# A fused attention and mixture-of-experts kernel: the order of eight row gathers, three table scatters, one table read and one weight load

## The chip, the cores and the metric

The kernel runs on one core of a Trainium2 chip. The metric is device time in microseconds, as the median of three runs. Engines are named as in the profile: PE is TensorE, DVE is VectorE, ACT is ScalarE, POOL is GpSimd, SP is SyncE, which only issues DMAs.

## What is computed

The first part is a retention layer: blockwise attention with a decay, over 4 batches, 8 heads, 768 positions and 64 channels. Its output is turned into `x`, 3072 rows of 512. The second part is a mixture of 8 experts in which every row goes to the one expert with the largest logit:

```python
logits = x @ w_gate
e_idx = np.argmax(logits, axis=1)
...
gate_w = probs[np.arange(N), e_idx]
eom = 1.0 / (1.0 + np.exp(-(x @ w_output_gate)))
for e in range(E):
    mask = e_idx == e
    h = np.maximum(x[mask] @ w1[e], 0.0)
    ye = h @ w2[e]
    out[mask] = gate_w[mask, None] * eom[mask, e, None] * ye
```

Which rows an expert gets is known only while the kernel runs, so the kernel sorts rows by expert in a table in DRAM and gathers them.

## The kernel before

**Attention and routing.** `x` is made in 24 tiles of 128 rows, by a software pipeline over steps s = -2 to 21 with the stages `stage_a` to `stage_d2`, and the last two tiles behind the loop. `stage_d2` turns a tile for DRAM and `store_x` sends two tiles at a time to `x_d` on SP's queue. Four tiles (the last four in two pairs) are routed together: `logits`, `route_choose` (which expert), `route_place` (which place in the table). For every tile `place_scatter` then writes 128 records of 12 bytes into the table `tab_d` with an indirect DMA from POOL. Each indirect DMA is made by POOL's own instruction (lines 712 and 969). `pace(t)` is a copy of one element on POOL that makes it wait for `t`, and `idle_for(2)`, a rest pair, two such copies of nothing in particular.

**The first expert.** After 16 tiles (`RES = 16`), the expert that has most rows so far is chosen, and its rows are worked on first, as "expert 0". Its rows among the first 16 tiles, the early rows, stand in the first 256 places of its list: eight gathers of 32 places each, in blocks 0 to 7, read from `x_d` into the tiles `xg(0, 0)` and `xg(0, 1)`. `x_turn(0, 0)` and `x_turn(0, 1)` transpose these on DVE, line 986, and PE's first expert products need them (`units`, issued by `fill`, line 1021: 16 units with the first tile, 16 with the second, 16 with both and the second half of the weights, `load_piece(1)`; then 16 units of second products with pieces 2 and 3, lines 84 to 86). Its places from 256 on, blocks 8 to 13, are shared between rows of the first 16 tiles, which come out of the table by `load_rows(0, 2)` (SP, line 869) and `row_index(0, 2)` (DVE, lines 897 and 902), and rows of the last 8 tiles, which PE finds by products with `marks` (`found`, lines 611 and 612; DVE, `row_turn` and `row_join`). The gathers 8 to 13 follow, and behind them those of expert 1, whose list is read by `load_rows(1)` and `row_index(1)` after all 24 scatters.

**What sets the order.** The block stands under `manual_schedule`: each engine, and each DMA queue, runs its instructions in the order of the program. The framework adds the waits from what is read and written. Accesses to `tab_d` are kept in program order among reads and scatters; scatters among themselves are declared free of order (`scatter`, line 722). On POOL, before the change: scatter of tile 12 (s = 17), gathers 0 and 1 (s = 18), 2 and 3 (s = 19), scatters of tiles 13 and 14 (s = 20), scatter of tile 15 and gather 4 (s = 21), gathers 5, 6 and 7 behind the loop, then the scatters of tiles 16 to 23 with a rest pair ahead of each, the gathers 8 to 13, and expert 1's. On SP: `load_piece(0)` (s = 19), stores, then at s = 21 `load_rows(0, 2)` and `load_piece(1)`, the last stores, `load_piece(2)` and `load_piece(3)`, `load_rows(1)`. On DVE, `row_index(0, 2)` stands ahead of the routing of the last two tiles and of `x_turn(0, 1)`; `row_index(1)` stands behind the split of the first quarter of piece 3 and ahead of its other three (lines 139 and 1470).

Of the kernel before, what the change touches and what calls it, by code (L numbers as in the profile page):

```python
# [25 lines left out]
def kernel(  # L26
# [17 lines left out]
    P = 128  # L44
# [31 lines left out]
    RES = 16  # L76
    def bank(name):
        return psum.tile([P, 512], F32, tag="bank", name=name)
# [627 lines left out]
    def place_scatter(count, rests=0):  # L706
        for _ in range(min(count, len(pending))):
            idx, rec = pending.pop(0)
            idle_for(rests)
            scatter(  # L710
                "table",
                nc.gpsimd.indirect_dma_start(  # L712
                    out=tab_d,
                    out_offset=bass.IndirectOffsetOnAxis(ap=idx, axis=0),
                    in_=rec,
                    in_offset=None,
                    bounds_check=P * E * EB - 1,
                    oob_is_err=False,
                ),
            )  # L720

    def scatter(group, ins):
        inst = getattr(ins, "ins", ins)
        tc.declare_no_dep(inst, group=group, reason="these scatters write different rows")
        tc.add_to_no_dep_group(group, inst)
# [137 lines left out]
    def load_rows(p, j0=0, j1=None, eng=nc.sync):  # L863
        if p >= E:
            return
        n = (KT[p] if j1 is None else j1) - j0
        t = const.tile([32, 4 * n, 3], I32, name=f"index_{p}_{j0}")
        src = tab_q[bass.ds(expert[p], 1)][:, :, 4 * j0 : 4 * (j0 + n), :]
        eng.dma_start(t, src.rearrange("e r j t -> (e r) j t"))
        idxs[(p, j0)] = (t, n)  # L870
# [17 lines left out]
    def idle_for(count):  # L888
        for _ in range(count):
            pace(warm[0:1])  # L890

    def row_index(p, j0=0):
        if p >= E:
            return
        t, n = idxs[(p, j0)]
        gf = const.tile([32, 4 * n], F32, name=f"rowf_{p}_{j0}")
        nc.vector.scalar_tensor_tensor(
            out=gf, in0=t[:, :, 2], scalar=float(4 * NT), in1=t[:, :, 2], op0=ALU.is_lt, op1=ALU.mult
        )
        gi = const.tile([P, 4 * n], I32 if p else F32, name=f"rows_{p}_{j0}")  # L900
        for qq in range(4):
            nc.vector.tensor_scalar(
                out=gi[32 * qq : 32 * qq + 32], in0=gf, scalar1=float(P * qq), scalar2=None, op0=ALU.add
            )
        if p == 0:
            part0[j0] = gi
            return
        for b in range(4 * n):
            gis[(p, 4 * j0 + b)] = gi[:, b : b + 1]
# [52 lines left out]
    def gather(p, b0=0, b1=None, rows=NT, rests=0):  # L962
        if p >= E:
            return
        for b in range(b0, NB[p] if b1 is None else min(b1, NB[p])):
            idle_for(rests)
            if (p, b // 4) not in xg:
                xg[(p, b // 4)] = slot(f"xg_{p}_{b // 4}")
            nc.gpsimd.indirect_dma_start(  # L969
                out=xg[(p, b // 4)][:, (b % 4) * P : (b % 4 + 1) * P],  # L970
                out_offset=None,
                in_=x_q[0 : 4 * rows],
                in_offset=bass.IndirectOffsetOnAxis(ap=gis[(p, b)], axis=0),
                bounds_check=4 * rows - 1,
                oob_is_err=False,
            )
# [301 lines left out]
    with tc.manual_schedule():  # L1278
# [13 lines left out]
        for s in range(-2, NTILE - 2):  # L1292
            if s >= 0:
                load_up_to(s + AHEAD - (s >= B), 2 if s < RES + 3 else 1)
            if s == -2:
                decay_table()
            if s == 0:
                stage_b(1)
                stage_b2(1)
            if s == RES + 1:  # L1300
                load_every()
            rest = stage_a(s + 2)
            if late:
                late.pop(0)()
            if s >= 1 and s % B == 0:
                logits(s - B, B)
            for f in rest:
                f()
            if s >= 0:
                stage_c1(s)  # L1310
            stage_a2(s + 2)
            if s + 1 >= 0 and s != 0:
                stage_b(s + 1)
            if s == RES + 2:
                pfound = bank("pfound")
                for b in range(B):
                    found(pfound, RES - B + b, 0, 2 * P, b == 0, b == B - 1)
                row_turn(0, pfound, 2 * P)
            n = s - 1
            if s >= 1 and s % B == 0:  # L1320
                logit_rows(s - B)
            if s + 1 >= 0 and s != 0:
                stage_b2(s + 1)
            if n >= 0 and n % B == B - 1:
                at_once(route_choose(n + 1 - B, n + 1))
                if n < RES:
                    pace(routed[n + 1 - B][0][0:1, 0, 0:1])
                else:
                    decay_queries(s + 2)
                ranking = route_place(n + 1 - B, n + 1)  # L1330
                per_turn[0] = 3 if n >= RES - 1 else 2
            if s == RES + 2:
                first_index()
                row_join(0, 2 * P)
            if s == RES + 5:
                decay_queries(s + 2)
            stage_k(s + 2)
            if s == RES + 1:
                weave(len(later))
                expert_regs(0, order_i, 1)  # L1340
            if s >= RES + 2:
                if s > RES + 2:
                    pace(live[s + 1]["at"][1][0:1, 0, 0:1])
                if s < RES + 4:
                    gather(0, 2 * (s - RES - 2), 2 * (s - RES - 2) + 1, RES * P)
                else:
                    place_scatter(1)
            if 0 <= n < LAST:
                stage_d2(n)
            if s in STORES:  # L1350
                store_x(STORES[s], 2)
            if s == 0:
                later.extend(inter_tables())
                routing_tables()
                order_tables()
            if s == 1:
                weave(len(later))
            if s == 2:
                nc.scalar.dma_start(wgs[:, :, 0:E], w_gate.rearrange("(c p) e -> p c e", p=P))
                nc.scalar.dma_start(wgs[:, :, E : 2 * E], w_output_gate.rearrange("(c p) e -> p c e", p=P))  # L1360
                blank_rows()
            if s == 5:
                number_tables()
            if s in EARLY_RECORDS:
                early_record(*EARLY_RECORDS[s])
            if s >= 0:
                stage_c(s)
            if s == RES + 3:
                decay_queries(s + 2)
            if ranking:  # L1370
                first_steps = pick_first() if s == RES else []
                late.append(lambda fs=first_steps[:1] + ranking[:1]: [f() for f in fs])
                place_scatter(len(pending) if s == RES else 0)
                later.extend(first_steps[1:] + ranking[1:-1])
                if s == RES:
                    later.extend(lambda b=b: mark(RES - B, b, 0, 2 * P) for b in range(B))
                later.extend(ranking[-1:])
                ranking = []
            if s == RES + 3:
                load_piece(0)  # L1380
            if s > RES:
                pace(xTs[s][0:1, 256:257])
                if s in (RES + 1, RES + 4):
                    place_scatter(1)
                elif s < RES + 4:
                    gather(0, 2 * (s - RES - 2) + 1, 2 * (s - RES - 2) + 2, RES * P, 2)
                else:
                    load_rows(0, 2)
                    load_piece(1)
                    gather(0, 4, 5, RES * P)  # L1390
            if s < RES:
                place_scatter(1 if s < RES - 2 else 2)

# [4 lines left out]
        weave(2)  # L1398
        stage_b2(n)
        pace(live[n]["at"][1][0:1, 0, 0:1])  # L1400
        gather(0, 5, 6, RES * P)
        stage_c(n - 1)
        pace(xTs[n - 1][0:1, 256:257])
        gather(0, 6, 7, RES * P)
        logits(LAST, 2)
        weave(len(later))
        for b in range(B):
            mark(RES, b, 1, late_width)
        gather(0, 7, 8, RES * P, 2)
        stage_c1(n)  # L1410
        logit_rows(LAST)
        stage_c(n)
# [11 lines left out]
            mark(LAST, b, 1, late_width)  # L1424
        stage_d2(n - 3, 2)
        fill(8)
        row_index(0, 2)
        logit_rows(LAST + 2)
        fill(8)
        at_once(route_choose(LAST + 2, NTILE))  # L1430
        x_turn(0, 1)
        stage_d2(n - 1, 2)
        load_piece(2)
        load_piece(3)
        last = route_place(LAST + 2, NTILE)
# [288 lines left out]
```

## Time and profile before

| | |
|---|---|
| median of 3 runs | 411.56 us (410.62 to 412.21) |
| the profiled execution's own time | 411.95 us |
| its span | 410.1 us |
| PE busy | 393.6 us, 96% |
| DVE, ACT, POOL busy | 289.0, 184.6, 245.7 us |
| chain that ended last | PE 77%, DMA 10%, SP's queue 6%, DVE 4% |

A row of the timeline gives the start, the length, the engine, the source line, the operation, what it writes and reads, the number of instructions merged into it and, in brackets, how long the engine sat idle just before and what ended that. A wait for several semaphores is put down to the one that came last by the profile; where the engine named had long been done, it was another, often a DMA. A granted clock of 1.00 is 2.4 GHz, 0.50 is 1.2 GHz.

### The profile page before, as it was taken

To read this page: it belongs to the slowest core of one execution; us is meant where nothing else is said; L and a number is where in the kernel's file an instruction comes from. 1 tells how busy PE (TensorE), PEld (TensorE's weight loads), DVE (VectorE), ACT (ScalarE), POOL (GpSimd) and SP (SyncE) were. 2 spreads that over 40 slices of the span, in tenths; PEclk is the share of its full clock that TensorE was granted. 3 is DMA by queue.
4 is the path that set the end of the run, shared out by engine and by line. 5 is a ranking of instruction groups with operands and counts; after the bars stand their busy time and mean duration, and the time that the engine had idled before them with its cause. 6 is when DMAs were issued, how large, how long until landed. Compare 5 with 4: busy or idle time off the path is not lost.

```text
span 410.1 us, 10897 instructions
## 1 busy us (share of the span) xinstructions
PE 393.6 (96%) x3847; PEld 368.6 (90%) x3847; DVE 289.0 (70%) x845; ACT 184.6 (45%) x450; POOL 245.7 (60%) x362
## 2 busy tenths in 40 slices
PE   7999999999959999999999999999999999999994
PEld 4888978888749899899999999999999999999984
DVE  3857686789964836875969858966976886875611
ACT  3767556687411504544435414704623642552500
POOL 2567886764876888686585656557466475403102
PEclk9999999999997999999999999999999999999999
DMA  9998999988867248754359646946965884783201
GB/s 183 226 208 209 246 252 241 258 223 207 270 185 245 58 164 258 229 197 144 129 167 307 225 141 197 307 144 180 320 214 151 270 301 135 229 318 111 71 26 49
DMA packets 106286, 81.99 MB, mean 200 GB/s; under 512 B 67028, under 2 KB 81386, under 8 KB 106210
## 3 DMA queue, kind: packets, MB, share of 16 engines
q1 hardware_dynamic: 97666, 67.52, 57.4%
q0 software_dynamic: 6288, 13.12, 10.0%
q8 instruction: 52, 0.85, 0.9%
q10 hardware_dynamic: 2256, 0.30, 0.5%
q14 instruction: 24, 0.20, 0.1%
HBM read 63.78 MB, written 17.55 MB: 198 GB/s over the span
## 4 chain that ended last, share of the span: by engine, by line
PE 77%; DMA 10%; SPq 6%; DVE 4%; POOL 1%; issue 1%; ACT 0%; POOLq 0%; ACTq 0%
PE ph L835 29%; PE py L835 25%; PE ph L1021 6%; DMA qkv<-in_v_dram 3%; SPq L178 3%; PE pyr L85 2%; PE pyr L84 2%; PE pyr L86 2%; SPq L171 2%; DMA qkv<-in_q_dram 2%; PE ps L392 2%; DMA xg<-x_d,rows 2%; DVE at L401 1%; PE po L436 1%; DMA qkv<-in_k_dram 1%
## 5 line engine op out<-in xcount | busy, mean ns | idle before, releaser
L969 POOL DMA_INDIRECT xg<-x_d,rows x103 | 116.2, 1128 | 53.2 <-issue 28.5
L1040 ACT ACTIVATE hhi<-ph 128x400 fp32r<-128x400 f32 (+6 forms) x72 | 33.7, 469 | 137.8 <-PE ph L835 108.6
L139 DVE TENSOR_TENSOR wlo<-raw,whi 128x512 fp32r<-128x512 f32 x120 | 79.8, 684 | 0.2
L835 PE MATMUL ph<-xhi,whi 128*128 128x400 f32 (+4 forms) x224 | 75.8, 339 | 0.3 <-PE py L835 0.3
L835 PE MATMUL ph<-xhi,wlo 128*128 128x422 f32 (+6 forms) x224 | 75.5, 337 | 0.0
L835 PE MATMUL ph<-xlo,whi 128*128 128x422 f32 (+6 forms) x224 | 75.3, 336 | 0.0
L130 ACT CAST whi<-raw 128x512 fp32r<-128x512 f32 x120 | 70.2, 614 | 4.7 <-DMA raw<-in_moe_w_dram 4.7
L835 PE MATMUL py<-hhi,whi 128*128 128x400 f32 (+9 forms) x192 | 65.2, 339 | 0.0
L835 PE MATMUL py<-hhi,wlo 128*128 128x422 f32 (+5 forms) x192 | 65.0, 338 | 0.0
L835 PE MATMUL py<-hlo,whi 128*128 128x422 f32 (+5 forms) x192 | 64.9, 338 | 0.0
L1046 DVE SCALAR_TENSOR_TENSOR hlo<-ph,hhi 128x400 fp32r<-128x400 f32 (+6 forms) x72 | 37.1, 519 | 34.8 <-ACT hhi L1040 34.1
L401 DVE TENSOR_TENSOR at<-ps,decay 128x512 f32<-128x512 f32 x48 | 31.3, 684 | 20.8 <-PE ps L392 19.6
L835 PEld LDWEIGHTS ph<-xhi,whi 128*128 128x128 f32 x224 | 42.1, 188 | 0.7 <-issue 0.5
L835 PEld LDWEIGHTS ph<-xlo,whi 128*128 128x128 f32 x224 | 42.2, 188 | 0.2
L835 PEld LDWEIGHTS ph<-xhi,wlo 128*128 128x128 f32 x224 | 42.1, 188 | 0.2
L835 PEld LDWEIGHTS py<-hlo,whi 128*128 128x128 f32 x192 | 36.2, 188 | 0.2
L835 PEld LDWEIGHTS py<-hhi,wlo 128*128 128x128 f32 x192 | 36.1, 188 | 0.2
L835 PEld LDWEIGHTS py<-hhi,whi 128*128 128x128 f32 x192 | 36.0, 188 | 0.1
L352 ACT COPY qT<-pq 64x256 f32<-64x256 f32 x88 | 34.7, 394 | 1.5 <-PE pq L344 0.6
L1021 PE MATMUL ph<-y,raw 128*128 128x128 f32 (+2 forms) x160 | 28.5, 343 | 4.7 <-DVE y L986 4.6
L712 POOL DMA_INDIRECT tab_d<-rec,idx x24 | 24.6, 1027 | 12.7 <-issue 5.8
L1021 PEld LDWEIGHTS ph<-y,raw 128*128 128x128 f32 x160 | 26.5, 214 | 6.0 <-DVE y L986 4.7
(216 smaller groups left out, 665.0 us busy)
## 6 DMA issues: line engine op xcount, KB each, us to landing
raw<-in_moe_w_dram SPq DMA_DIRECT2D x32, 1024.0 KB
x_d<-xn SPq DMA_DIRECT2D x12, 512.0 KB
qkv<-in_k_dram SPq DMA_DIRECT2D x38, 128.0 KB
qkv<-in_v_dram SPq DMA_DIRECT2D x19, 256.0 KB
qkv<-in_q_dram SPq DMA_DIRECT2D x36, 128.0 KB
yd<-yo SPq DMA_DIRECT2D x17, 256.0 KB
yr<-yd SPq DMA_DIRECT2D x68, 64.0 KB
xg<-x_d,rows POOLq DMA_INDIRECT x103, 3.4
```

What stands on the lines that cost most here:

```text
L84: nc.tensor.matmul(ps, a[0], b[0], start=first, stop=False)
L130: nc.scalar.copy(out=hi, in_=src)
L139: eng.tensor_tensor(out=lo, in0=src, in1=hi.bitcast(F32), op=ALU.subtract)
L178: eng.dma_start(t.rearrange("p (m y) d -> p y m d", y=2)[:, y], rows[:, 4 * y : 4 * y + 4])
L352: copies = [lambda r=r, view=view, src=src: nc.scalar.copy(out=view(qT[r]), in_=src) for r, view, src in query_parts(pq)]
L401: nc.vector.tensor_tensor(out=at, in0=ps.rearrange("p (g t) -> p g t", g=NPAIR), in1=dec[:, j], op=ALU.mult)
L712: nc.gpsimd.indirect_dma_start(out=tab_d, out_offset=bass.IndirectOffsetOnAxis(ap=idx, axis=0), in_=rec, in_offset=None, bounds_check=P * ...
L835: nc.tensor.matmul(ps[:, 0:m], a[x], b[y][:, 0:m], start=first and i == 0, stop=last and i == 2)
L969: nc.gpsimd.indirect_dma_start(out=xg[(p, b // 4)][:, (b % 4) * P : (b % 4 + 1) * P], out_offset=None, in_=x_q[0 : 4 * rows], in_offset=ba ...
L1021: nc.tensor.matmul(phs[(p, fc)][:, r].rearrange("p (b r) -> p b r", b=nb), raws[fc // 4][:, kc, sl], ys[(p, h)][:, y0 : y0 + nb * P].rearr ...
L1040: nc.scalar.activation(out=hi[:, r], in_=ph[:, r], func=AF.Relu)
L1046: nc.vector.scalar_tensor_tensor(out=to, in0=ph[:, r], scalar=0.0, in1=hi[:, r].bitcast(F32), op0=ALU.max, op1=ALU.subtract,)
```

## The change

All eight gathers of early rows now stand in the steps s = 18 to 21, two in each, the second of each step with a rest pair ahead (before, gathers 1, 3 and 7 had one). The scatters of tiles 13, 14 and 15 move behind them, after the loop, the last with a rest pair. `load_piece(1)` moves to s = 20, ahead of the table's read; `load_rows(0, 2)` moves behind the scatter of tile 15, after the loop; `row_index(0, 2)` moves behind `x_turn(0, 1)` and the last `stage_d2`. No operation is added or left out but rest pairs: one more ahead of gather 5 and one ahead of tile 15's scatter.

```diff
--- before.py
+++ after.py
@@ -1341,10 +1341,7 @@
             if s >= RES + 2:
                 if s > RES + 2:
                     pace(live[s + 1]["at"][1][0:1, 0, 0:1])
-                if s < RES + 4:
-                    gather(0, 2 * (s - RES - 2), 2 * (s - RES - 2) + 1, RES * P)
-                else:
-                    place_scatter(1)
+                gather(0, 2 * (s - RES - 2), 2 * (s - RES - 2) + 1, RES * P)
             if 0 <= n < LAST:
                 stage_d2(n)
             if s in STORES:
@@ -1380,14 +1377,12 @@
                 load_piece(0)
             if s > RES:
                 pace(xTs[s][0:1, 256:257])
-                if s in (RES + 1, RES + 4):
+                if s == RES + 1:
                     place_scatter(1)
-                elif s < RES + 4:
+                else:
                     gather(0, 2 * (s - RES - 2) + 1, 2 * (s - RES - 2) + 2, RES * P, 2)
-                else:
-                    load_rows(0, 2)
+                if s == RES + 4:
                     load_piece(1)
-                    gather(0, 4, 5, RES * P)
             if s < RES:
                 place_scatter(1 if s < RES - 2 else 2)
 
@@ -1398,15 +1393,16 @@
         weave(2)
         stage_b2(n)
         pace(live[n]["at"][1][0:1, 0, 0:1])
-        gather(0, 5, 6, RES * P)
+        place_scatter(1)
         stage_c(n - 1)
         pace(xTs[n - 1][0:1, 256:257])
-        gather(0, 6, 7, RES * P)
+        place_scatter(1)
         logits(LAST, 2)
         weave(len(later))
         for b in range(B):
             mark(RES, b, 1, late_width)
-        gather(0, 7, 8, RES * P, 2)
+        place_scatter(1, 2)
+        load_rows(0, 2)
         stage_c1(n)
         logit_rows(LAST)
         stage_c(n)
@@ -1424,12 +1420,12 @@
             mark(LAST, b, 1, late_width)
         stage_d2(n - 3, 2)
         fill(8)
-        row_index(0, 2)
         logit_rows(LAST + 2)
         fill(8)
         at_once(route_choose(LAST + 2, NTILE))
         x_turn(0, 1)
         stage_d2(n - 1, 2)
+        row_index(0, 2)
         load_piece(2)
         load_piece(3)
         last = route_place(LAST + 2, NTILE)
```

## Rows read from the trace of the kernel before

**Rows 1.** Page, part 1: busy us (share of the span) and instructions, PE.

```profile
PE 393.6 (96%) x3847; PEld 368.6 (90%) x3847; DVE 289.0 (70%) x845; ACT 184.6 (45%) x450; POOL 245.7 (60%) x362
```

**Rows 2.** Timeline of PE: start, us, what, count [idle before <-releaser].

```profile
122.86 2.08 PE L1021 MATMUL ph<-y,raw 128*128 128x128 f32 x8 [4.55 <-DVE y L986]
...
130.47 0.25 PE L611 MATMUL pfound_late<-marks,row_lo 128*128 128x192 bf16 x1
```

**Rows 3.** Stretches of 1 us: length, PE busy, granted clock, DMA share, GB/s.

```profile
122.00:123.00 1.00, 0.14 (x1) 0.56 0.22 79
...
128.00:129.00 1.00, 1.00 (x7) 0.53 0.95 272
129.00:130.00 1.00, 1.00 (x9) 1.00 0.93 287
```

**Rows 4.** Timeline of DVE, 94 to 160 us.

```profile
116.94 0.12 DVE L897 SCALAR_TENSOR_TENSOR rowf<-index 32x8 f32<-32x8 int32 x1
...
122.09 0.71 DVE L986 STREAM_TRANSPOSE y<-xg 128x512 f32<-128x512 f32 x1 [3.00 <-DMA xg<-x_d,rows]
...
125.12 0.18 DVE L672 TENSOR_TENSOR pr<-pr,ebase 128x16 f32<-128x16 f32 x1 [1.13 <-PE pr L642]
...
125.77 0.57 DVE L604 TENSOR_SCALAR marks<-slot_no,lead,sl 128x192 bf16<-128x192 bf16 x2
...
139.60 0.16 DVE L897 SCALAR_TENSOR_TENSOR rowf<-index 32x16 f32<-32x16 int32 x1
...
140.53 1.90 DVE L139 TENSOR_TENSOR wlo<-raw,whi 128x512 fp32r<-128x512 f32 x3
```

**Rows 5.** Timeline of POOL, 105 to 160 us.

```profile
109.77 0.98 POOL L712 DMA_INDIRECT tab_d<-rec,idx  x1 [0.16 <-issue]
...
114.89 0.41 POOL L886 COPY beat<-warm 1x1 f32<-1x1 f32 x2
115.84 1.02 POOL L969 DMA_INDIRECT xg<-x_d,rows  x1 [0.54 <-issue]
...
117.94 1.04 POOL L712 DMA_INDIRECT tab_d<-rec,idx  x1 [0.65 <-issue]
...
131.96 0.98 POOL L712 DMA_INDIRECT tab_d<-rec,idx  x1 [0.57 <-issue]
...
140.02 1.00 POOL L969 DMA_INDIRECT xg<-x_d,rows  x1 [0.30 <-issue]
...
159.96 1.02 POOL L969 DMA_INDIRECT xg<-x_d,rows  x1 [0.16 <-issue]
```

**Rows 6.** Chain that ended last, in order of time: start, us, what.

```profile
115.84 6.23 DMA xg<-x_d,rows
...
138.03 0.23 PE pyr L84
...
148.93 10.40 PE ph L1021 x64
...
168.48 18.50 PE ph L835 x96
```

**Rows 7.** Tile xg, gathers of 136 to 141 us: issue to landing.

```profile
DMA to landing us min/median/max: 3.3/3.3/3.3
```

**Rows 8.** Waits of SP's queue: total us, times, longest.

```profile
SPq L869 <- DMA tab_d<-rec,idx: 7.9, 1, 7.9
```

**Rows 9.** Timeline of SP: the two reads of the table's rows.

```profile
115.01 0.36 SPq L869 DMA_DIRECT2D index<-tab_d  x1
...
135.76 0.34 SPq L869 DMA_DIRECT2D index<-tab_d  x1
```

**Rows 10.** Timeline of POOL, 76 to 95 us: tile 11's scatter, read, tile 12's scatter.

```profile
82.05 1.01 POOL L712 DMA_INDIRECT tab_d<-rec,idx  x1 [0.17 <-issue]
...
88.80 0.70 POOL L918 DMA_DIRECT2D every<-tab_d  x1 [1.97 <-DMA tab_d<-rec,idx]
...
94.34 1.07 POOL L712 DMA_INDIRECT tab_d<-rec,idx  x1 [2.40 <-PE po L436]
```

## The prediction

> **What bounds the kernel now.** I read the page's busy table first: PE is at work 96% of the span [rows 1], so only what moves a stop of PE, or its clock, moves the end. The timeline of PE then shows one large stop, 4.55 us ahead of 122.86, released by DVE's transpose of the gathered rows (tile y, line 986) [rows 2]. The clock table shows a second price: the granted clock is at half (1.2 of 2.4 GHz) from that stop on, 0.53 as the mean of 128 to 129 and 1.00 after it [rows 3], so until about 128.94. That is 6.08 us at half speed, 3.04 us lost. The stop costs 4.55 + 3.04 = 7.6 us. DVE's timeline says why: x_turn(0, 1) at 122.09 sat 3.00 us for the DMA of a gather [rows 4], and POOL's timeline says why that was late: gather 7 starts at 115.84, behind the scatters of tiles 13 to 15, the last at 109.77 [rows 5]. POOL is a single file of descriptors from 105 to 160 us, with no long waits.
>
> **Rows of the first gathers.** The change takes three scatters out of the way of gathers 4 to 7. A rest pair costs 114.89 to 115.84, 0.95 us [rows 5]. Gather 5 gets one, and so gather 7 stands three DMAs earlier and one pair later, near 113, and lands, even with the 6.23 us that the old one took from issue to landing [rows 6], by 119.2; with 3.3 us [rows 7] by 116.3. DVE would have come to x_turn(0, 1) at 122.09 - 3.00 = 119.1, and at 118.2 without row_index(0, 2), which moves behind it (0.93 us, 139.60 to 140.53 [rows 4]). PE can go on at about 119.0 instead of 122.86: 3.9 us won. A stop of 0.7 us remains; I take it that the clock holds through so short a one, 3.0 us more. PE's work from 122.86 to the found matmuls at 130.47 [rows 2] is 7.61 us, 4.57 at full clock: it wants them at 123.6.
>
> **The piece of weights.** load_piece(1) leaves SP near 105 instead of behind the table's read. It is first used by the matmuls after the found ones, so its 1 MB has over 15 us; it competes with gathers 4 to 7, whose slack is the 1.9 us between 116.3 and 118.2 and then the 3.9 us won. I cost it at nothing; with that cover gone it would cost at most the 3.9.
>
> **The table's read, the step that turns the sum.** load_rows(0, 2) must follow the scatters of tiles 12 to 15, and every later scatter into tab_d must follow the read: only scatters among themselves are declared free (line 724). Before, SP sat 7.9 us for the scatter [rows 8], the read left at 115.01 [rows 9] and had landed by 116.94, where DVE used it without a wait [rows 4]; scatter 16 came only at 117.94, so nothing showed. That a scatter waits for a read shows elsewhere: the read of the whole table leaves POOL at 88.80 and the next scatter is held until 94.34, 2.40 us after POOL was free [rows 10]; PE, named there, writes nothing that it needs.
> Now tile 15's scatter is the seventh DMA in the file, where gather 7 was, with two more rest pairs: 115.84 + 2 x 0.95 = 117.74. Its landing is not in the trace. Near rows: at most 3.80 us (scatter 23 at 131.96, the read that needs it at 135.76), 5.24 (this scatter, 109.77 to 115.01), 6.75 (scatter 11, 82.05 to 88.80) [rows 5, 9, 10]. Gathers in a quiet stretch land in 3.3 [rows 7]. The queues are emptier at 118 than at 110, so I take 3.80, and 3.3 to 6.75 as the ends. The read's own time is at most 1.93 (115.01 to 116.94); I take that. So the read has landed at 117.74 + 3.80 + 1.93 = 123.47, and scatter 16 starts there and not at 117.94: **+5.56 us** for everything behind it on POOL, eight scatters, gathers 8 to 13 and expert 1's gathers.
> The Trainium skill, in "DMA: Bandwidth & Descriptors", section "Anatomy of one DMA — SWDGE (gpsimd) path", gives about 2.0 us of fixed time to such a DMA, most of it the wait until the last byte is confirmed in HBM. This case's 3.8 to 6.75 us are above that. By 2.0 the sum would be the third rival's.
>
> **What is late next.** Three chains come back to PE.
> (a) row_index(0, 2) now stands on DVE ahead of the last tiles' slots and marks. 123.47 + 0.93 = 124.40; slots to marks took 125.12 to 126.34 [rows 4], 1.22: found matmuls at 125.6, not 123.6. They started at 130.47 and the second weights' products at 138.03 [rows 2, 6]: 7.56 on, 133.2.
> (b) Scatter 23 moves to 137.5. The read of expert 1's rows, which left at 135.76 [rows 9], waits for it: 141.3, landed 143.25, row_index(1) done 144.2. Behind row_index(1) on DVE stand three splits of weights' piece 3, 1.90 us [rows 4]; the first is done at 144.8. The 16 units of second products take 138.03 to 148.93 [rows 6], 0.681 each; the tenth, which needs that split, is due at 133.2 + 9 x 0.681 = 139.3. PE stops 5.5 us. The one stop of 4.55 us halved the clock for 6.08 us, so this longer one should: 3.04 lost again. Seven units are left: 144.8 + 4.77 + 3.04 = 152.6 for what started at 148.93: **+3.7 us**.
> (c) Gather 13 moves from 140.02 to 145.6, is landed at 148.9 and turned by 149.3, ahead of 152.6. Expert 1's last gather moves from 159.96 to 165.5 [rows 5]; landed 168.8, with transpose, row_index and split (0.4 + 0.93 + 0.3) ready at 170.4, while PE comes to it at 168.48 [rows 6] + 3.7 = 172.2. Neither adds.
> From 168.48 PE runs without a stop worth the name to the end, so 3.7 us stay. The profiled run's time is 411.95 us (span 410.1, and 1.85 around it), which makes 415.65; it stands 0.39 over the median 411.56, so on the median **415.3 us**.
>
> **The rivals.**
> 1. The clock stays up after the second stop, or the stop is broken up enough: 144.8 + 4.77 = 149.6, and then chain (c) is last, 170.4 against 168.48: +1.9, 413.5. For it: only one stop of this kind is in the trace. Against: that one was shorter. Chance 0.12.
> 2. Scatter 15 lands as slowly as scatter 11, 6.75: 2.95 us more on the whole chain, 418.2. For it: piece 1 and the x_d stores now sit in the queues just before. Against: the 3.80. Chance 0.14.
> 3. Both scatters land in 2.0 us, well under the shortest landing shown: scatter 16 at 121.7, scatter 23 at 135.7, first split at 141.2. The tenth unit is due at 137.5, a stop of 3.7; without a fall of the clock PE is 2.9 us ahead, but expert 1's rows are ready at 168.6: +0.2, about 411.7. The 3.3 us of a gather [rows 7] speak against it. It is what the Trainium skill's page named above would give. Chance 0.08.
> 4. **Not slower**: scatter 16 is not held by the read (its wait falls on what had landed anyway). It starts a rest pair behind scatter 15, 119.7, +1.8; scatter 23 at 133.75, first split at 141.0, the stop is 1.7, PE is 145.8 against 148.93, 3.1 ahead, and expert 1's rows let it keep 1.8: 409.8. It decides once scatter 16 starts before about 121.5, where (c) would meet 168.48. The 2.40 us at 94.34 speak against it. Chance 0.08.
>
> **How the numbers follow.** Forecast 0.58, rivals 0.12, 0.14, 0.08, 0.08. A difference under 0.5%, 2.06 us, is about what a measurement can't tell from none. Faster by more (under 409.5): half of rival 4, 0.04. Within: 0.04 of rival 4, 0.08 of rival 3, 0.08 of rival 1, 0.03 of the forecast, 0.23. Slower: the rest, 0.73. The range goes from 411.3 (rival 3 in) to 418.5 (rival 2 in); rival 4 and a slow landing of both scatters (+9.6) stay out.
>
> **What would show it.** PE's stop at 118 under 1.5 us, no half clock until 138; the table's read leaving SP at 121 to 122.5; scatter 16 at 123 to 124; a new stop of PE of 4 to 7 us near 139, released by a split of weights (line 139), with the clock at half behind it; line 1021's last 64 matmuls starting near 152.6. Wrong if scatter 16 starts by 121, if the stop stays under 3 us, or if the clock holds through it.

## Result and profile after

The changed kernel takes 414.86 us (median of 6 runs, 413.73 to 415.47) against 411.56 us for the kernel before (6 runs): ratio 1.0082, 95% interval 1.0061 to 1.0103. It is slower by 0.8%. A ratio here compares the undisturbed runs of a kernel with those of the kernel before on the same chip, and so differs a little from the quotient of the medians. The profiled execution took 414.8 us, its span is 413.0 us. In a second set of runs, below, the same kernel came to 1.0088 (1.0057 to 1.0120).

The page's busy table, as [rows 1]: of the 2.9 us that the span is longer, PE is busy for 1.7 and idle for 1.2, with the same 3847 instructions.

```profile
PE 395.3 (96%) x3847; PEld 367.6 (89%) x3847; DVE 287.2 (70%) x845; ACT 185.3 (45%) x450; POOL 248.1 (60%) x366
```

The timeline of PE, as [rows 2]:

```profile
120.46 1.16 PE L1021 MATMUL ph<-y,raw 128*128 128x128 f32 x8 [0.65 <-DVE y L986]
...
144.02 0.79 PE L85 MATMUL pyr<-wlo,hhi 128*128 128x512 f32 x1 [4.85 <-DVE wlo L139]
...
151.39 10.56 PE L1021 MATMUL ph<-y,raw 128*128 128x192 f32 x64
...
171.68 0.35 PE L835 MATMUL ph<-xhi,whi 128*128 128x432 f32 x1
```

The stop of 4.55 us is down to 0.65, and a stop of 4.85 us ends 23.6 us later, released by the split of piece 3. Stretches of 1 us with columns as in [rows 3]: the clock was at 1.00 through the short stop, fell to half in the long one, near 143.0, and was back at 1.00 near 149.8 (a mean of 0.58 from 149 to 150).

```profile
120.00:121.00 1.00, 0.54 (x4) 1.00 0.00 0
...
142.00:143.00 1.00, 0.00 (x0) 1.00 0.35 67
143.00:144.00 1.00, 0.00 (x0) 0.51 0.20 66
...
149.00:150.00 1.00, 1.00 (x4) 0.58 0.05 12
150.00:151.00 1.00, 1.00 (x6) 1.00 0.19 66
```

POOL's timeline, as [rows 5] (tile 15's scatter, tile 16's, tile 23's, gather 13, and the eighth gather of expert 1):

```profile
118.22 0.98 POOL L712 DMA_INDIRECT tab_d<-rec,idx  x1 [0.57 <-issue]
...
123.33 0.98 POOL L712 DMA_INDIRECT tab_d<-rec,idx  x1 [3.72 <-DMA index<-tab_d]
...
137.79 0.98 POOL L712 DMA_INDIRECT tab_d<-rec,idx  x1 [0.57 <-issue]
...
145.75 1.00 POOL L969 DMA_INDIRECT xg<-x_d,rows  x1 [0.30 <-issue]
...
156.62 1.02 POOL L969 DMA_INDIRECT xg<-x_d,rows  x1 [0.16 <-issue]
```

SP's timeline gives the two reads of the table, as [rows 9], and the weight pieces 4 and 5:

```profile
120.34 0.35 SPq L869 DMA_DIRECT2D index<-tab_d  x1
...
139.93 0.34 SPq L869 DMA_DIRECT2D index<-tab_d  x1
...
150.10 1.04 SPq L117 DMA_DIRECT2D raw<-in_moe_w_dram  x2
```

DVE's timeline, as [rows 4]: the transpose of the early rows has no wait any more, the index waits 0.99 us for the read; the last row is the transpose of expert 1's second tile, x_turn(1, 1).

```profile
119.69 0.71 DVE L986 STREAM_TRANSPOSE y<-xg 128x512 f32<-128x512 f32 x1
122.58 0.16 DVE L897 SCALAR_TENSOR_TENSOR rowf<-index 32x8 f32<-32x8 int32 x1 [0.99 <-DMA index<-tab_d]
...
163.20 0.71 DVE L986 STREAM_TRANSPOSE y<-xg 128x512 f32<-128x512 f32 x1 [2.93 <-DMA xg<-x_d,rows]
```

The chain that ended last, as [rows 6]: start, us, what. Before, it was PE without a break from 122.86 on. Now it runs through tile 23's scatter, the read behind it, DVE's index, POOL's gathers from 143.04 on, the landing of the one at 156.62, DVE, and only then PE.

```profile
137.79 2.12 DMA tab_d<-rec,idx
139.93 2.13 DMA index<-tab_d
...
156.62 6.45 DMA xg<-x_d,rows
...
171.84 4.25 PE ph L835 x22
```

Releasers in such a chain are inferred. POOL's timeline shows no wait for the read of expert 1's rows: its index was ready by 143.3, the first gather that uses it started at 147.07, behind gather 13, and the fourteen gathers from 139.08 to 156.62 stand 1.30 to 1.41 us apart. So what made the eighth gather of expert 1 late is the file on POOL itself. What joins that gather to PE is DVE's order: the last operations `hlo` of expert 0, which PE's second products read, stand behind its transpose, and PE waits for one of them:

```profile
167.34 0.50 PE L86 MATMUL pyr<-whi,hlo 128*128 128x512 f32 x1 [0.17 <-DVE hlo L1046]
```

Three rows of the kernel before that the prediction did not read are wanted beside these. POOL's, DVE's and PE's timeline: the eighth gather of expert 1, its transpose, and the first products of line 835.

```profile
151.25 1.02 POOL L969 DMA_INDIRECT xg<-x_d,rows  x1 [0.16 <-issue]
...
159.12 0.71 DVE L986 STREAM_TRANSPOSE y<-xg 128x512 f32<-128x512 f32 x1 [1.47 <-DMA xg<-x_d,rows]
...
168.32 0.36 PE L835 MATMUL ph<-xhi,whi 128*128 128x432 f32 x1
```

The eighth gather is 5.37 us later than before, x_turn(1, 1) 4.08, the first L835 3.36, the end of the span 2.9. But the first expert product was itself 1.50 us later in this trace (115.89 for 114.39). Counted from there, the three are 3.87, 2.58 and 1.86 us later.

### The profile page after: what moved, and what is told of

Same layout as the page of the kernel before. It is cut to its first block, busy times and chain, and to the rows that moved or that the text cites. A ratio compares the mean times of both kernels' runs of the same rounds, so it can differ in the third digit from the quotient of the medians.

```text
span 413.0 us, 10903 instructions
## 1 busy us (share of the span) xinstructions
PE 395.3 (96%) x3847; PEld 367.6 (89%) x3847; DVE 287.2 (70%) x845; ACT 185.3 (45%) x450; POOL 248.1 (60%) x366
## 4 chain that ended last, share of the span: by engine, by line
PE 73%; DMA 10%; DVE 5%; POOL 5%; SPq 4%; issue 2%; POOLq 0%; ACTq 0%; ACT 0%; DVEq 0%
PE ph L835 29%; PE py L835 25%; DMA qkv<-in_q_dram 4%; PE po L436 3%; PE ps L392 3%; POOL xg L969 2%; SPq L178 2%; PE po L416 2%; DMA q<-in_q_dram 2%; DMA xg<-x_d,rows 2%; DMA qkv<-in_v_dram 2%; SPq L171 1%; PE pl L484 1%; PE pq L344 1%; PE ph L1021 1%
## 5 line engine op out<-in xcount | busy, mean ns | idle before, releaser
L835 PE MATMUL ph<-xhi,whi 128*128 128x400 f32 (+4 forms) x224 | 75.8, 338 | 0.0
L835 PE MATMUL ph<-xhi,wlo 128*128 128x422 f32 (+6 forms) x224 | 75.4, 337 | 0.0
L835 PE MATMUL ph<-xlo,whi 128*128 128x422 f32 (+6 forms) x224 | 75.3, 336 | 0.0
L835 PE MATMUL py<-hhi,whi 128*128 128x400 f32 (+9 forms) x192 | 65.2, 339 | 0.0
L835 PE MATMUL py<-hhi,wlo 128*128 128x422 f32 (+5 forms) x192 | 65.0, 338 | 0.0
L835 PE MATMUL py<-hlo,whi 128*128 128x422 f32 (+5 forms) x192 | 64.9, 338 | 0.0
L835 PEld LDWEIGHTS ph<-xhi,whi 128*128 128x128 f32 x224 | 42.1, 188 | 0.5 <-issue 0.3
L835 PEld LDWEIGHTS ph<-xlo,whi 128*128 128x128 f32 x224 | 42.1, 188 | 0.2
L835 PEld LDWEIGHTS ph<-xhi,wlo 128*128 128x128 f32 x224 | 42.1, 188 | 0.2
L835 PEld LDWEIGHTS py<-hlo,whi 128*128 128x128 f32 x192 | 36.1, 188 | 0.2
L835 PEld LDWEIGHTS py<-hhi,wlo 128*128 128x128 f32 x192 | 36.0, 188 | 0.2
L835 PEld LDWEIGHTS py<-hhi,whi 128*128 128x128 f32 x192 | 36.0, 188 | 0.2
L1021 PE MATMUL ph<-y,raw 128*128 128x128 f32 (+2 forms) x160 | 25.7, 318 | 0.8 <-DVE y L986 0.7
L1148 POOL DMA_INDIRECT out_dram<-yo,outrow x9 | 10.0, 1115 | 27.2 <-DVE yo L1132 22.4
```

Of the source, the lines that this page charges most:

```text
L835: nc.tensor.matmul(ps[:, 0:m], a[x], b[y][:, 0:m], start=first and i == 0, stop=last and i == 2)
L1021: nc.tensor.matmul(phs[(p, fc)][:, r].rearrange("p (b r) -> p b r", b=nb), raws[fc // 4][:, kc, sl], ys[(p, h)][:, y0 : y0 + nb * P].rearr ...
```

## One table for all traces

Every trace gives the same few starts (us). "First" is the first expert product of line 1021; "stops" are PE's idle times near 120 and near 140; "last 64" the last 64 matmuls of line 1021; "turn" is x_turn(1, 1).

| kernel | first | stops | last 64 | turn | L835 | L835 - last 64 | L835 - turn | span |
|---|---|---|---|---|---|---|---|---|
| before | 114.39 | 4.55, none | 148.77 | 159.12 | 168.32 | 19.55 | 9.20 | 410.1 |
| changed | 115.89 | 0.65, 4.85 | 151.39 | 163.20 | 171.68 | 20.29 | 8.48 | 413.0 |
| c0_after_again | 114.11 | 0.65, 4.65 | 148.29 | 161.98 | 170.36 | 22.07 | 8.38 | 411.8 |
| c6_busy_stop | 115.86 | 0.65, 0.29 | 150.04 | 163.89 | 172.30 | 22.26 | 8.41 | 413.8 |
| c5_other_table | 116.39 | 0.65, 3.34 | 149.32 | 161.99 | 170.64 | 21.32 | 8.65 | 412.1 |
| c1_piece_early | 115.65 | 2.30, none | 146.89 | 161.52 | 170.05 | 23.16 | 8.53 | 411.7 |
| e2_piece_early_index_late | 116.34 | 0.86, 1.23 | 147.30 | 161.85 | 170.34 | 23.04 | 8.49 | 411.6 |
| e4_after_no_rests | 116.01 | 0.65, none | 145.15 | 158.46 | 166.92 | 21.77 | 8.46 | 408.2 |
| e8_before_no_rests | 115.98 | 2.57, none | 145.55 | 154.79 | 165.10 | 19.55 | 10.31 | 406.3 |
| e7_early_no_rests | 116.44 | 0.79, none | 144.22 | 155.40 | 163.76 | 19.54 | 8.36 | 405.2 |

Three things are read from it. From L835 to the end of the span every kernel takes 241.2 to 241.8 us, so the start of L835 decides. From the last 64 to L835 PE needs 19.55 us when nothing holds it (before, e8, e7). From the turn to L835 it can't be less than 8.36 to 8.65 us: wherever the first difference is above 19.55, the second is in that band. So two chains meet at L835, PE's own and the rows of expert 1, and the table says for each kernel which one came last. In the kernel before PE's came last, but only by 9.20 less that floor, 0.6 to 0.8 us.

"First" differs by up to 2.3 us between traces, and by 1.8 us between the two of the same kernel (changed and c0): that belongs to the stage ahead, so single traces are compared by differences inside them, and times by the medians. No effect of the change shows in it: the five traces with the new order have a mean "first" of 115.65, the five with the old one 115.76. Each row is one execution, and not always a middling one: the one of c5 took 413.91 us for a median of 412.31, the one of e8 408.16 for 410.55.

## Experiments

**The change itself again (c0_after_again),** on the chip of c5, c1 and e7. (c6, e2, e4 and e8 ran on another, on which the changed kernel was not run; there it is compared by the ratios.)

> The changed kernel itself, as the measure for the others of this call: about 0.8% over the kernel before. On the chip of the first four runs PE came to the first expert products some 4 us later and then sat for instructions between 150 and 170 us; here both theories expect only that the stop near 139 has its length by how much later PE comes: 4.8 us less that delay.

414.54 us, 1.0088 (1.0057 to 1.0120). The stops repeat. The half clock does only in part: it lasted from about 141.5 to 144.9 here, 3.4 us, where the other trace has 6.8. L835 stood all the same 8.38 us behind the turn.

**The hold alone (c5_other_table).** The read of the table is pointed at a second, blank table that no scatter writes, so nothing behind it is held. The kernel then leaves out the early rows of expert 0 from place 256 on; it makes as many gathers.

```diff
-        src = tab_q[bass.ds(expert[p], 1)][:, :, 4 * j0 : 4 * (j0 + n), :]
+        part = tab_q if j0 == 0 else tab_e.rearrange("(j r e) t -> e r j t", r=32, e=E)
+        src = part[bass.ds(expert[p], 1)][:, :, 4 * j0 : 4 * (j0 + n), :]
```

> The changed kernel with the table's read taken from a second, blank table (the early rows of expert 0 from place 256 on are left out of its first products), against the changed kernel of this call. Theory of the hold: scatter 16 starts about 2 us behind scatter 15 instead of 5.1, the stop near 139 shrinks by about 3 us and the clock holds where it fell; 0.7 to 1.1% faster than the changed kernel where that stop is 4.8 us long, no difference where it is not there. Rival (attention stage): within 0.3% of the changed kernel in any case.

412.31 us, 1.0011 (0.9989 to 1.0034): 0.8% faster than the changed kernel by the ratios, 2.2 us by the medians. POOL's timeline (line 712 is 714 in this kernel) has tile 16's scatter 1.97 us behind tile 15's, where the changed kernel has 5.11:

```profile
119.75 0.98 POOL L714 DMA_INDIRECT tab_d<-rec,idx  x1 [0.57 <-issue]
121.72 0.98 POOL L714 DMA_INDIRECT tab_d<-rec,idx  x1 [0.57 <-issue]
```

So the hold is real and is nearly all that the change loses; without it the change is no gain either. Up to that stop PE and SP kept their times: counted from "first", pieces 2 and 3 leave SP after 6.28 us and the found matmuls come after 9.34 us in this kernel, in c0 and in the changed one. Part of the expectation missed: the stop near 140 fell to 3.34 us only, and the clock still fell in it.

**The second stop kept busy (c6_busy_stop).** Is the half clock behind the stop a price?

```diff
-        fill(4)
+        fill(1)
+        idle2 = bank("idle2")
+        for _ in range(20):
+            nc.tensor.matmul(idle2, blank[:, 0:P], blank, start=True, stop=True)
+        fill(3)
```

> The changed kernel with 20 extra matmuls of a zero tile put into PE's queue just ahead of the split-bound second products (in the fill ahead of row_index(1)'s splits), so that PE has something to do in its stop near 140 us. They leave the output as it is. Theory (the stop's second price is the half clock behind it): the granted clock stays at 1.00 from 138 to 152, the last 64 matmuls of line 1021 start 1.5 to 3 us earlier than in the changed kernel, 0.4 to 0.7% are won, ratio to the kernel before 1.001 to 1.005. Rival 1 (the clock is no price, only the stop is): ratio 1.007 to 1.011 as the changed kernel. Rival 2 (the added matmuls delay the real ones, 20 x 0.21 us with the stop as cover only in part): 1.009 to 1.015.

416.43 us, 1.0097 (1.0067 to 1.0127): nothing won. PE's 1-us stretches stay at 1.00 from 138 to 154, the split releases PE at 143.78 (144.02 in the changed kernel), so the theory got its clock. But PE then waits for gather 13, and expert 1's rows are no earlier. PE's and DVE's timeline:

```profile
143.78 0.50 PE L85 MATMUL pyr<-wlo,hhi 128*128 128x512 f32 x1 [0.29 <-DVE wlo L139]
...
150.04 10.64 PE L1021 MATMUL ph<-y,raw 128*128 128x192 f32 x64 [1.40 <-DVE y L986]
...
163.89 0.71 DVE L986 STREAM_TRANSPOSE y<-xg 128x512 f32<-128x512 f32 x1 [4.80 <-DMA xg<-x_d,rows]
```

Both traces have the same "first" to 0.03 us. The last 64 start 1.35 us earlier, L835 0.62 later. My expectation missed; that the clock is no price is what the run says, for this kernel, since the rows of expert 1 cover it.

**The piece of weights alone (c1_piece_early).** The kernel before with load_piece(1) at s = 20.

```diff
                     load_rows(0, 2)
-                    load_piece(1)
                     gather(0, 4, 5, RES * P)
+                if s == RES + 4:
+                    load_piece(1)
```

> The kernel before with load_piece(1) alone moved to s = 20. Theory A (piece 1 beside it made gather 7 land late): PE's stop ahead of the second tile's products falls from 4.55 to under 2 us and the clock holds: 0.5 to 1% faster than the kernel before. Theory B (the scatters ahead of the gathers made them late): the stop stays over 3.5 us, within 0.2% of the kernel before.

412.64 us, 1.0028 (1.0011 to 1.0045). The first stop halves, to 2.30 us, and yet the kernel is not faster: the turn waits 5.68 us for its gather, at 161.52, and L835 follows 8.53 behind. x_turn(0, 1) waits for no gather here: what is left of the first stop comes from DVE's own order, which e2 changes. And the early piece has a price that the kernel before does not pay. The table's read left SP 6.08 us behind scatter 15 (5.91 in e2, 5.94 in e7, DMA share over 1.00 until 115 in all three) where before it was 5.24 and in e8 3.63, and so the hold shows in the old order too. POOL's timeline:

```profile
119.69 1.04 POOL L712 DMA_INDIRECT tab_d<-rec,idx  x1 [1.22 <-DMA index<-tab_d]
```

Counted from "first", the eighth gather of expert 1 started 1.3 us later than in the kernel before. Scatter 16 accounts for 0.5 of that; between 132 and 142 some POOL instructions took longer besides (gathers of 1.23 to 1.45 us for 1.0), for a cause that no run shows.

**The piece and the index (e2_piece_early_index_late).** As c1, and row_index(0, 2) behind x_turn(0, 1).

```diff
-        row_index(0, 2)
         logit_rows(LAST + 2)
...
         stage_d2(n - 1, 2)
+        row_index(0, 2)
```

> The kernel before with the second weights' piece asked for at s = 20, ahead of the table's read, and row_index(0, 2) behind x_turn(0, 1); all gathers, scatters and rest pairs stay in the old order. It is e7_early_no_rests with the rest pairs put back. Theory A (the two moves take the stop near 118 away, but the chain of scatters with rest pairs gives it back at expert 1's rows): stop at 118 to 122 under 1.5 us, clock 1.00, scatter 23 at 131 to 133, DVE's x_turn(1, 1) waits 4 to 6 us for its gather, PE's small waits in 161 to 168 add 1 to 3 us; 409 to 412, ratio 0.994 to 1.001. Rival B (rest pairs cost nothing; the two moves are the whole of what e7_early_no_rests won): 406.5 to 408.5, ratio 0.987 to 0.993.

414.36 us, 1.0045 (1.0019 to 1.0071): worse than either theory. The first stop is 0.86 us at full clock; all of it is given back. The chain shows gather 7 landing in 2.56 us, behind the same three scatters as before, and DVE's timeline has one of the two longest waits of the turn:

```profile
117.76 2.56 DMA xg<-x_d,rows
...
161.85 0.71 DVE L986 STREAM_TRANSPOSE y<-xg 128x512 f32<-128x512 f32 x1 [5.60 <-DMA xg<-x_d,rows]
```

**The same without rest pairs ahead of scatters 16 to 23 (e7_early_no_rests).**

```diff
-        place_scatter(len(pending), 2)
+        place_scatter(len(pending))
```

in its three places.

> The kernel before, with load_piece(1) at s = 20, row_index(0, 2) behind x_turn(0, 1), and no rest pairs ahead of the scatters of tiles 16 to 23. The order of gathers and scatters is that of before, so the read of the table does not come late; without the 8 rest pairs (0.95 us each) scatter 23 and all behind it on POOL come some 6 to 7.6 us earlier than before. If the chain through scatter 23, the read of expert 1's rows and the splits behind it is what limits once the stop at 118 is gone, this is faster than moving the piece alone: 1 to 1.6% faster than the kernel before, 405 to 407.5 where that takes 411.6. If the rest pairs keep something else going (descriptors on POOL beside DVE, or the DMAs of the last stores), it is no faster than moving the piece alone.

407.00 us (6 runs, 405.46 to 407.94), 0.9890 (0.9860 to 0.9920): faster than both kernels, as expected. The turn and L835 on DVE's and PE's timeline:

```profile
155.40 0.71 DVE L986 STREAM_TRANSPOSE y<-xg 128x512 f32<-128x512 f32 x1 [2.30 <-DMA xg<-x_d,rows]
...
163.76 0.36 PE L835 MATMUL ph<-xhi,whi 128*128 128x432 f32 x1
```

Here both chains arrive together: 19.54 behind the last 64, 8.36 behind the turn.

**The rest pairs alone (e8_before_no_rests).** The three lines above in the kernel before.

> The kernel before without the rest pairs ahead of scatters 16 to 23 alone; the piece of weights and the table's index stay where they were. Theory A (what e7_early_no_rests won came from the stop near 118, which the place of the piece and of the index set, and from the short chain of scatters together): the stop of 4.55 us near 118 stays with its half clock, nothing else is late, so at most the small waits of 150 to 170 go: 409.5 to 411.5, ratio 0.995 to 1.000. Rival B (the rest pairs alone were the price, and the stop's time is given back because expert 1's rows come early): 406.5 to 408.5, ratio 0.987 to 0.993.

410.55 us, 0.9947 (0.9916 to 0.9978): between the two theories. It is also a second look at the first stop, since this program equals the kernel before up to scatter 16. PE's timeline:

```profile
122.47 1.16 PE L1021 MATMUL ph<-y,raw 128*128 128x128 f32 x8 [2.57 <-DVE y L986]
```

2.57 us and a granted clock of 1.00 in every stretch from 114 to 154, where [rows 2, 3] show 4.55 and half clock: gather 7 was turned 4.29 us after its start here, 6.25 there [rows 4, 5]. So some of the 7.6 us that I meant to win belonged to that one execution; two traces do not tell how much is usual.

**The changed kernel without rest pairs (e4_after_no_rests),** nine pairs, from scatter 15 on.

```diff
-        place_scatter(1, 2)
+        place_scatter(1)
```

and the three lines above.

> The changed kernel without the rest pairs ahead of the scatters of tiles 15 to 23 (nine pairs of about 0.95 us). Theory A (what costs time in the changed kernel is that the whole POOL chain behind scatter 16 is late, and PE meets it at the splits near 140): scatter 15 starts about 117, the read leaves about 119.3, scatter 16 about 122.3, scatter 23 about 7 us earlier than in the changed kernel, 130 to 131, read of expert 1's rows 132 to 133; no stop of PE near 140, no half clock; expert 1's first gathers land before PE wants them; 406 to 409, ratio 0.987 to 0.994. Rival B (the rest pairs protect transfers: without them the scatters crowd the queues and the table's read and the weights land late): landing of scatter 15 above 4 us, scatter 16 later than 124, ratio 1.005 or more. Rival C (the hold of scatter 16 is the price by itself): ratio about 1.003 to 1.006.

411.36 us, 0.9974 (0.9943 to 1.0004), by the ratios 1.1% below the changed kernel. Theory A's 406 to 409 is missed. As it says, the stop near 140 and the half clock are gone; as it does not say, gather 13 stops PE for 1.31 us and the turn still waits 4.35 for its gather, 8.46 ahead of L835. Landing of scatter 15: 2.11 us (118.69 to the read at 120.80), so the rest pairs protected nothing there (rival B falls).

**The piece behind the read (e3_piece_behind),** and first runs of e1, e5 and e6 (the kernels that c1, c5 and c6 repeat), all on a chip on which the kernel before took 424.56 us, PE came to the first products at 119.5 to 122.6 and sat for its own instructions between 150 and 170, so that only what happens before 150 is read from these.

```diff
-                if s == RES + 4:
-                    load_piece(1)
...
         load_rows(0, 2)
+        load_piece(1)
```

> The changed kernel, but load_piece(1) stands behind load_rows(0, 2) in SP's queue, as before the change. Theory of the hold: piece 1 leaves near 120.7 instead of 107.55 and lands near 125.5, about when the first matmuls with it are due; up to 1.5 us of a stop of PE there, which the later stop (set by scatter 23, not moved) takes up: 414.5 to 416. Rival (piece 1 among the last loads of the attention stage is what makes that stage 1.5 us later): the first expert products start near 114.4 and the time is 413 to 413.5.

425.93 us, 1.0041 (1.0010 to 1.0072). Behind the read the piece leaves SP at 122.40, and PE waits 0.65 us for it, at 128.90. So in the new order the early piece saves at least this wait. What it is worth in time is not shown: the changed kernel was not run on this chip.

> The changed kernel, with the read load_rows(0, 2) taken from a second table that no scatter writes (blank: the early rows of expert 0 from place 256 on are left out of its first products; as many gathers are made). Theory of the hold: the read neither waits for tile 15's scatter nor holds tile 16's. Scatter 16 starts a rest pair behind scatter 15, near 120.2 instead of 123.33, scatter 23 near 134.7, the first split of piece 3 behind row_index(1) near 140.9; PE's stop near 139 falls from 4.8 to under 2.5 us and the clock stays at 1.00; the last 64 matmuls of line 1021 start near 145.5 instead of 151.39, expert 1's rows then end last: about 410 to 411 us. Rival (the attention stage, whose first expert products start at 115.89 instead of 114.39, is what costs): the stop may go, but the time stays within 1 us of the changed kernel's 414.9.

424.72 us, 0.9998 (0.9965 to 1.0030), not the 410 to 411 expected: scatter 16 stands 1.97 us behind scatter 15 here too, but the time can't be read on this chip.

> The kernel before, with load_piece(1) alone moved to s = 20, ahead of the table's read. Theory A (gather 7 landed late, 6.2 us after its start at 115.84, because piece 1 left at 115.57 beside it): it lands in 3.3 to 4.2 us, near 119.5; PE's stop at 118 falls from 4.55 to under 2 us, the clock stays at 1.00; the scatters of tiles 16 to 23 stay where they were, near 118 to 132; the end is set by what follows them: 408 to 409.5 us. Theory B (the scatters ahead of gathers 4 to 7 made them late, as the prediction has it): the stop stays over 3.5 us and the time within 0.8 us of 411.6.

423.31 us, 0.9977 (0.9948 to 1.0005); the first stop was 1.36 us.

> The changed kernel, with 20 matmuls on a blank tile (128 x 512 bf16, some 4.3 us in all) put where PE stops near 139; nothing waits for them. Theory (the stop costs its length and then half the clock for 6 us): the stop stays, as these matmuls, but the granted clock stays at 1.00; the last 64 matmuls of line 1021 start 3.0 us earlier, near 148.4, and the end is 1.5 to 3 us earlier, 412 to 413.4, as expert 1's rows let it. Rival (the clock costs nothing here because something else is late by as much): 414.9, no change.

428.46 us, 1.0105 (1.0068 to 1.0141): PE was so late that no stop was left for the added matmuls to fill; it tells nothing of the clock, and c6 repeats it.

## Why the prediction was right, and where it was not

415.3 us was forecast and 414.86 measured. The sign and the first cause of the loss were right, the read that holds POOL's file; the step that carried the sum to the end was not the one that did it, and that the number came so close is in part luck (see (c)).

- **Rows of the first gathers.** The size was right: stop 0.65 for 0.7, clock 1.00. The cause was not: the three scatters ahead of gather 7 were taken for what made it late, but in e2 they stand there still and the stop is 0.86. Gather 7 landed in 2.56 us there and in 2.49 in e7, where piece 1 had left SP over 10 us earlier, and in 6.23 in the kernel before, where piece 1 left SP at 115.57 beside it. In e8, with piece 1 beside it at 115.51, it took 4.27. So moving all eight gathers, which sent the table's read behind them, was not needed for this stop. And what the stop was worth was not asked. By the table, the kernel before had 0.6 to 0.8 us to win at L835 before expert 1's rows would have been last. The 6.9 us of the sum at 118 could not have come through, whatever became late next, and c1 and e2 show the gain vanish there. The prediction took chain (c) from expert 1's last gather, and so did not see that slack. The rival "not slower" gave it 1.8 us.
- **The piece of weights.** Right at nothing, as far as it shows, in the new order, where scatter 15 lands in 2.12 us. In the old order the landing is slower in each of the three traces with an early piece (c1).
- **The table's read.** Scatter 16 at 123.47 forecast, 123.33 measured, but by terms that cancel. Scatter 15 started at 118.22 for 117.74, in a run whose attention was 1.5 us late. It landed in 2.12 us, for 3.80. From the read's issue to POOL's start went 2.99, for 1.93: DVE used what was read 2.24 after the issue, POOL's write was let go 0.75 later still. Counted from "first", the hold made scatter 16 later by (123.33 - 115.89) - (117.94 - 114.39) = 3.89 us, where 5.56 was forecast (5.53 by its own terms); c0 gives 3.88. Of that c5 took away 3.14 (5.11 - 1.97).
- **The landing.** The Trainium skill, in "DMA: Bandwidth & Descriptors", section "Anatomy of one DMA — SWDGE (gpsimd) path", gives about 2.0 us of fixed time, which I had set aside as too short for these rows. The trace agrees with it in the quiet stretches (2.12 and 2.14 us for scatters 15 and 23, with a DMA share of 0.00 to 0.05), and not in the loaded ones (5.24 and 6.75 in [rows 9, 10], 6.45 for the gather at 156.62). The 3.80 that I took as the nearest row was not a landing. The waits of SP's queue in the kernel before, from 95 to 140 us, show only one for a scatter, the 7.9 us of [rows 8] that the first read waits; ahead of the second, at 135.76, SP waits for DVE's line 808, a step of choosing expert 1, which was done at 135.05:

```profile
SPq L765 <- DVE rows_i L808: 9.1, 1, 9.1
```

Where SP did wait for scatter 23, the same read left 6.55 us behind it in e8 (127.75 to 134.30, DMA share 0.46 to 1.07 until 134), 2.15 in e4 and 2.14 in the changed kernel (DMA share at most 0.06). So it is the load beside it that goes with a long landing.

- **(a) The found matmuls.** Wrong: they did not wait for the marks and came 9.34 us behind "first", at PE's own pace. With the index in DVE's hands at 122.58, the prediction's own 0.93 and 1.22 give marks at 124.7, ahead of PE at 125.23.
- **(b) The stop.** Right in kind, place and releaser: 4.85 us at 139.2 for 5.5 at 139.3, half clock for 5.8 us behind it, last 64 later by 2.6 for 3.7. But counted from "first" the last 64 are later by 1.1, and in c0, with a stop of 4.65, they are 0.2 earlier than before. And c6 takes the clock out and c5 a third of the stop, and only c5, which also brings POOL's file forward, changes the time. The stop is a sign of the late file and not the loss.
- **(c) Expert 1's rows.** "Neither adds" is the step that failed. It followed the last gather, with the 3.3 us of a quiet stretch. The eighth is the one that the second tile waits for, and it lands in 6.45 us, beside the 3 MB of pieces 4 to 6 (DMA share 0.99 to 1.25 from 152 to 162). PE's own chain would have been at L835 at 151.39 + 19.55 = 170.94; the rows let it start at 171.68. Counted from "first", L835 is 1.86 us later than before, and PE's own chain accounts for 1.12 of that. In c0 L835 is 2.32 later, and PE's own chain would have been 0.20 earlier than before: there the rows are the whole loss. So the 3.7 us were summed for a chain that was later by 1.1 us and by nothing, and the chain that was put at nothing cost 1.9 to 2.3. The medians are 3.3 and 2.7 us apart; what makes up the rest of that is not shown by one trace each.
- **The rivals.** Clock (rival 1): the clock fell, and c6 shows that its price here is nothing; but the end of that rival, chain (c) last and 1.9 us lost, is nearer to the traces than my own. Slow landing: no. The 2.0 us landing (rival 3) happened, and its 411.7 did not, because the read held POOL 1.06 us longer and the rows of expert 1 bound. Not held (rival 4): no; c5, where it is made true, took 412.31, for 409.8.

Where the change put its price is thus settled by c5 and e4: the file of indirect DMAs on POOL, from scatter 16 on. What stays open is why the eighth gather is turned only 6.1 us (e8, 148.67 to 154.79) to 7.9 us (before, 151.25 to 159.12) after its start; that the weights beside it are the cause is not shown, since no run took them away.

## What to carry to other kernels

Before counting a stop as gain, follow every consumer behind the same queue to the point where it meets the bound engine, and take the smallest distance there as the most that can be won; here it was 0.6 to 0.8 us of a stop that looked like 7.6. Move one thing at a time: the piece of weights and the index alone took the stop down to 0.86 us, without the late read. A read put between writes of one DRAM table holds them all, so it belongs where the queue has a pause anyway, or the queue behind it must be made shorter. Rest pairs and other spacing in a queue are worth a run without them each time the order changes: with them the early piece and index lost 0.45%; without them the kernel was 0.5% faster in the old order and 1.1% faster with the two moves.

## What was unexpected in the hardware

- After a stop of 2.30 us (c1) the granted clock was at half (0.50 to 0.52 from 122 to 125), after one of 2.57 us (e8) at 1.00. Stops of 0.65 to 1.44 us left it at 1.00 in every trace of the table, and 3.34 to 4.85 us halved it in each, for 3.4 to 6.8 us. Twenty matmuls of zeros in the stop kept it up (c6).
- The indirect scatter of tile 15 landed in 2.1 us in its new place, in the changed kernel and in e4 alike; in its old place the read behind it left 3.63 us (e8, 111.32 to 114.95) to 6.08 us (c1, 110.97 to 117.05) after its start, the longer ones where piece 1 had left SP 4.6 to 5.9 us ahead of it.
- A gather of 32 rows landed in 2.56 us with a DMA share of 0.19 to 0.40 beside it (e2, gather 7, 117 to 120), in 6.23 with 0.64 to 1.07 (before, gather 7, 116 to 122) and in 6.45 with 0.99 to 1.25 (changed, the eighth of expert 1, 156 to 162).
- A write to a DRAM table behind a read of it began 2.99 us after the read's issue, 0.75 us after DVE had begun to use what was read (2.98 and 0.75 in c0, 2.71 and 0.75 in e4, 2.64 and 0.78 in c1).
